# The tail of a chunked attention and eight-expert MoE kernel laid out by hand, with VectorE turning the rows of six experts

## The chip, the cores and the metric

The kernel runs on one NeuronCore of a Trainium2 chip. The metric is device time in microseconds (us) of one execution, as a median over runs. A profiled execution is one more, with a trace of every instruction; its span goes from the first to the last instruction.

Engines: PE is TensorE (PEld its weight loads), DVE is VectorE, ACT is ScalarE, POOL is GpSimd, SP is SyncE, which here issues DMAs.

## The reference

Two stages, all in float32. First a chunked linear attention with decay over 4 x 8 heads, 768 tokens, head size 32, state size 16, in chunks of 32 (cut to what matters):

```python
cum = np.cumsum(log_a_chunk)                       # per head
M = (Cc @ Bc.T) * exp(cum_i - cum_j) * causal
y = M @ xc + (Cc @ state) * exp(cum)
state = exp(sum(log_a)) * state + (Bc * exp(cum_last - cum)).T @ xc
```

Its output, 3072 tokens of 256 values, goes through a mixture of experts with top-1 routing, 8 experts of 256 x 1024 x 256, and a capacity of 768 tokens for each, in the order of the tokens:

```python
e = argmax(x @ w_gate); gate = softmax(x @ w_gate)[e]
pos = how many earlier tokens chose e               # dropped where pos >= 768
out = gate * (relu(x @ w1[e]) @ w2[e])              # 0 where dropped
```

## The kernel before, in words

All engines' programs are written out in order by `moe_kernel` under a manual schedule; waits come from the tiles that instructions share. There is no planner: an instruction's place in the source is its place in its engine's queue.

**Attention.** 24 tiles of 128 tokens (`TILES`), six to a batch. The loop `for k in range(TILES + 1)` is a software pipeline. In step k, VectorE multiplies the scores of tile k by the decays (`masked`, tile `mz`, L436); TensorE turns the rows of tile k-2 and computes their logits (`rows_of`, `stage_c`), then does the products of tile k-1 (`intra` L451, `inter` L462, evicted by ScalarE as `ys`, L464), the state of tile k+1 (`carry`, tile `dsp`, L390, scaled by VectorE as `dsm`, L393) and, at the top of the next step, `scores` (L430). GpSimd prepares `bpt` and `ct` two tiles ahead.

**Routing.** Tiles are routed in groups (`GROUPS = [4, 4, 4, 4, 3, 2, 2, 1]`). `route_1` (VectorE: maximum, one-hot choice), `route_2` (TensorE: position of each token within its expert, tile `pos`), `route_3` (VectorE: gate, slot, one-hot tiles `hot_a`, `hot_e`; SP stores the rows to `rows_d` in HBM), `hot` (GpSimd) and `listed` (TensorE, added up in `table`). `route_1` and `route_3` put their VectorE operations in the list `side`; `trickle` runs five a step, `flush` runs all at once. A group that ends from step `LATE - 1` = 21 on, or at `LEAD` = 12, is flushed. From `table`, `numbers` makes `who`: for each expert and place, the token's number.

**Lead.** The first 128 tokens of expert 0 come from the first 12 tiles. They are fetched during the loop (`lead_gather`), turned after it (`lead_turn`) and go through w1 in eight pieces (`lead_gemm`, L622); w2 follows in the expert part (L987), with the turn of expert 0's other rows inside it (`TURN`).

**Experts.** `experts("first", ...)`: expert 0 with 296 rows, then experts 1 to 7 with 424 each. GpSimd fetches the rows by `who` in blocks of 128 (`gather`, `fetch`, L160), two experts ahead, each block released by a matmul of GEMM2. `turned` has TensorE turn them (`turn`, L150, eight transposes), ScalarE and VectorE split them in a high and a low part (`xh`, `xl`). GEMM1 (`gemm1`, L881) and GEMM2 (`gemm2`, L900) multiply high and low parts three ways. The weights are loaded by SP (`load_weights`, L105, L107) into one raw buffer for w1 and one for w2, as soon as the previous expert's are split (`split_weights`, ScalarE L121 and VectorE L122), which happens beside GEMM2. `finish` and `put` turn the result back, scale it by the gate and scatter it (GpSimd, L934). Expert 7 uses `gemm2_by_token` (L958). Expert 0's w1 is split in steps 19 to 22 of the loop (`SPLITS`), four pieces of 512 columns, its w2 after it.

**Rare part.** Under `tc.If` (L1044), for tokens beyond a window of 424 rows an expert or beyond the capacity: the same functions with `rare` set. With the inputs used it is not entered.

Of the kernel before, what the change touches and what calls it, by code (L numbers as in the profile page):

```python
# [18 lines left out]
P = 128  # L19
# [5 lines left out]
E = 8  # L25
# [8 lines left out]
GROUPS = [4, 4, 4, 4, 3, 2, 2, 1]  # L34
LEAD = 12
LATE = 22
WARM = 19
LOT = 4
TURN = (1, 4)
SPLITS = (19, 20, 21, 22)  # L40
# [13 lines left out]
def moe_kernel(ctx, tc, a, x, bt, bn, cn, hd, w_gate, w1, w2, cb, out, cap):  # L54
# [11 lines left out]
    ks = -(-cap // P)  # L66

# [30 lines left out]
    win = min(WIN, cap)  # L98
# [11 lines left out]
    def split_weights(e, r1, r2, wp, cuts=2):  # L110
        t = {}
        todo = []
        for nm, r in (("1", r1), ("2", r2)):
# [4 lines left out]
            m = n * r.shape[2] // cuts  # L118
            for i in range(cuts):
                def job(hi=flat(hi), lo=flat(lo), r=flat(r), sl=slice(i * m, (i + 1) * m)):  # L120
                    act.activation(hi[:, sl], r[:, sl], AF.Copy)  # L121
                    dve.tensor_tensor(out=lo[:, sl], in0=r[:, sl], in1=hi[:, sl].bitcast(F32), op=ALU.subtract)  # L122
                todo.append(job)
            t[nm] = (hi, lo)
        wset[e] = t
        return todo
# [25 lines left out]

    def follow(ins, name, reason):
# [12 lines left out]
    def numbers(out, cols):  # L166
        dve.scalar_tensor_tensor(out=out, in0=table[:, 0, cols], scalar=float(P), in1=table[:, 1, cols], op0=ALU.mult, op1=ALU.add)


    with ExitStack() as at:  # L170
# [356 lines left out]
        def route_2(n0, T, rt, df, ep, oh, se, soon=False):  # L527
            flush()
            act.activation(ep, df, AF.Exp)
            pos = p1.tile([P, T, E], F32, name="pos", tag="y" if soon else "sp", bufs=1 if soon else 2)  # L530
            pe.matmul(pos, tri, oh.rearrange("p t e -> p (t e)"), start=True, stop=False)
            pe.matmul(pos, ones, bc(runs[0].rearrange("p (o e) -> p o e", o=1), [P, T, E]), start=False, stop=T == 1)
            for i in range(1, T):
                pe.matmul(pos[:, i:T], ones, bc(oh[:, i - 1:i], [P, T - i, E]), start=False, stop=i == T - 1)
# [80 lines left out]
        lead_f = list(range(NF if lead else 0))  # L615

        def lead_gemm(n):
            for _ in range(min(n, len(lead_f))):
                f = lead_f.pop(0)
                ps = p1.tile([P, lead], F32, name="lead_p1", tag=("yp0", "yp1", "lj")[f % 3])  # L620
                for k in range(2):
                    pe.matmul(ps, rw[0][:, k, f * P:(f + 1) * P], lead_t["x"][:, k], start=k == 0, stop=k == 1)  # L622
                act.activation(lead_t["h"][:, f], ps, AF.Relu)
# [14 lines left out]
        def settle_due(now):  # L638
            while due and due[0][0] <= now < TILES - 0.5:
                _, group = due.pop(0)  # L640
                route_3(*route_2(*group, soon=True))
                if now > LATE - 1 or group[0] + group[1] == LEAD:
# [10 lines left out]
        def lot_of(n):  # L653
            gi = max(i for i in range(len(GROUPS)) if starts[i] <= n)
            T, i = GROUPS[gi], n - starts[gi]
            if T <= 2:
# [20 lines left out]
        for k in range(TILES + 1):  # L677
            b, t = divmod(k, NT)
            n = k - 2
            if k < TILES:  # L680
                ms[k] = masked(sps.pop(k) if k in sps else scores(k), lxs.pop(k))
# [4 lines left out]
            def rows_of(n, k):  # L686
                gi, i, direct, size = lot_of(n)
                if i == 0:
                    T = GROUPS[gi]
                    rt = sm.tile([P, 6, ROW], F32, name="rt", bufs=3) if T > 2 else sm.tile([P, T, ROW], F32, name=f"rt{gi}", bufs=1)  # L690
                    grp[gi] = rt, sm.tile([P, 6, E], F32, name="L", bufs=3)[:, 0:T]
                stage_c(sb[n], grp[gi][0], i, grp[gi][1], direct)
                lot = None
                if size:
                    lot = [sb[m] for m in range(n + 1 - size, n + 1)], grp[gi][1][:, i + 1 - size:i + 1]
                for f in full:
                    group_done(f, k)
                full.clear()
                if n + 1 == starts[gi + 1]:
                    if not direct:  # L700
                        full.append(gi)
                    else:
                        group_done(gi, k)
                return lot

            if n >= 0 and k < TILES:
                lot = rows_of(n, k)
            if k + 1 < TILES:
                lxs[k + 1] = decays(k + 1)
            if k >= 1:  # L710
                yps, lots = intra(x_of(k - 1), ms.pop(k - 1), sa[k - 1], lot, hots)
            if k + 1 < TILES:
                dsm = carry(k + 1)
# [4 lines left out]
            if k == TILES:  # L718
                rows_of(n, k)
# [9 lines left out]
            if k + 1 < TILES:  # L729
                sa[k + 1] = advance(k + 1, dsm)  # L730
            if lead and k == TILES:
                lead_turn()
# [38 lines left out]

        rt = sm.tile([P, 1, ROW], F32, name="rt_last", bufs=1)
        lg = stage_c_last(sb.pop(TILES - 1), rt)
        ops = take()
        for _, group in due[:-1]:
# [346 lines left out]
```

## Time and profile before

| | |
|---|---|
| median of 3 runs | 292.1 us (290.39 to 294.04) |
| profiled execution | 292.75 us |
| its span | 291.0 us |
| mean granted TensorE clock | 0.939 |
| busy, share of the span | PE 89%, PEld 74%, DVE 60%, ACT 45%, POOL 37% |
| DMA | 36.40 MB, mean 125 GB/s |

The page gives the span in 40 slices, so 7.3 us each; a digit is a tenth, of busy time or of the granted clock. Other views cut the span in stretches, list single instructions in order of time (start, length, engine, source line, tiles written and read), follow the chain of waits back from the last instruction, or group instructions by line. Matmul lengths are modelled and overlap, so that a busy TensorE is not TensorE at its peak.

### The profile page before, as it was taken

What the parts mean: (1) busy time and instruction counts of PE and PEld (TensorE: products, weight loads), DVE (VectorE), ACT (ScalarE), POOL (GpSimd) and SP (SyncE); (2) the same over time, 40 slices, a digit from 0 to 9 for tenths busy, and PEclk for the clock granted to TensorE, in tenths of its full rate; (3) what the DMA queues carried; (4) which work ended last, traced back from release to release, by engine and by line L of the source; (5) the groups of instructions that cost most, each with busy time, mean ns of one, the idle gap of its engine ahead of it and who ended that gap; (6) DMA issues with size and microseconds to landing.
All of it is one profiled execution on the core that took longest, in us unless ns stands there. A gap on an engine that the chain in (4) does not pass through costs nothing.

```text
span 291.0 us, 7064 instructions
## 1 busy us (share of the span) xinstructions
PE 258.1 (89%) x2768; PEld 215.4 (74%) x2768; DVE 174.6 (60%) x461; ACT 129.6 (45%) x290; POOL 107.0 (37%) x151
## 2 busy tenths in 40 slices
PE   7669999997988869799999999999999999999910
PEld 2235566654557758699999999999998999999900
DVE  7678797865875663476746736646656656645100
ACT  2458566564632342374644544544644635432000
POOL 6972324415102041555244335225325424042410
PEclk9999999999965795999999999999999999999975
DMA  6774527759112154227074173182271461001100
GB/s 187 169 213 103 169 71 202 235 143 337 43 41 93 55 187 141 84 63 305 16 216 169 33 247 140 31 304 78 67 284 47 119 233 51 2 18 42 38 27 0
DMA packets 14374, 36.40 MB, mean 125 GB/s; under 512 B 4621, under 2 KB 7919, under 8 KB 12288
## 3 DMA queue, kind: packets, MB, share of 16 engines
q1 hardware_dynamic: 10928, 28.18, 30.5%
q0 software_dynamic: 3280, 7.71, 8.1%
q8 instruction: 23, 0.38, 0.6%
q14 instruction: 15, 0.12, 0.1%
q10 hardware_dynamic: 128, 0.01, 0.0%
HBM read 29.29 MB, written 6.63 MB: 123 GB/s over the span
## 4 chain that ended last, share of the span: by engine, by line
PE 75%; DVE 11%; DMA 4%; ACT 2%; issue 2%; POOL 1%; SPq 0%; POOLq 0%; DVEq 0%; ACTq 0%
PE ps L881 25%; PE ps L900 22%; PE ps2f L958 4%; PE ps L150 3%; PE yp L451 3%; DMA g<-rows_d,who 3%; PE sp L430 2%; PE psy L946 2%; PE yp L462 2%; PE pj L469 2%; DVE mz L436 2%; PE dsp L390 2%; PE lead_p L622 1%; DVE state L417 1%; PE ldp L380 1%
## 5 line engine op out<-in xcount | busy, mean ns | idle before, releaser
L884 DVE SCALAR_TENSOR_TENSOR hl<-ps,hh 128x424 fp32r<-128x424 f32 (+1 forms) x64 | 37.3, 583 | 43.7 <-ACT hh L883 36.6
L160 POOL DMA_INDIRECT g<-rows_d,who x31 | 34.1, 1099 | 55.5 <-PE ps L900 43.5
L883 ACT ACTIVATE hh<-ps 128x424 fp32r<-128x424 f32 (+1 forms) x64 | 32.7, 511 | 46.7 <-PE ps L881 45.9
L122 DVE TENSOR_TENSOR wl<-r,wh 128x1024 fp32r<-128x1024 f32 (+1 forms) x36 | 38.2, 1099 | 17.8 <-ACT wh L121 17.8
L934 POOL DMA_INDIRECT out<-yo,oi x31 | 30.5, 985 | 43.3 <-DVE yo L933 38.2
L900 PE MATMUL ps<-hh,wh 128*128 128x424 f32 (+1 forms) x112 | 39.5, 352 | 0.0
L900 PE MATMUL ps<-hh,wl 128*128 128x424 f32 (+1 forms) x112 | 39.0, 348 | 0.0
L900 PE MATMUL ps<-hl,wh 128*128 128x424 f32 (+1 forms) x112 | 38.9, 347 | 0.0
L881 PE MATMUL ps<-xh,wh 128*128 128x424 f32 (+1 forms) x128 | 37.5, 374 | 0.0
L881 PE MATMUL ps<-xh,wl 128*128 128x424 f32 (+1 forms) x128 | 34.7, 353 | 0.0
L881 PE MATMUL ps<-xl,wh 128*128 128x424 f32 (+1 forms) x128 | 34.6, 352 | 0.0
L121 ACT ACTIVATE wh<-r 128x1024 fp32r<-128x1024 f32 (+1 forms) x36 | 32.7, 956 | 0.1
L881 PEld LDWEIGHTS ps<-xh,wl 128*128 128x128 f32 x128 | 24.2, 193 | 0.6
L881 PEld LDWEIGHTS ps<-xl,wh 128*128 128x128 f32 x128 | 24.1, 192 | 0.6
L881 PEld LDWEIGHTS ps<-xh,wh 128*128 128x128 f32 x128 | 22.3, 196 | 0.3
L900 PEld LDWEIGHTS ps<-hh,wh 128*128 128x128 f32 x112 | 21.0, 188 | 1.0
L900 PEld LDWEIGHTS ps<-hh,wl 128*128 128x128 f32 x112 | 21.2, 189 | 0.4
L900 PEld LDWEIGHTS ps<-hl,wh 128*128 128x128 f32 x112 | 21.0, 187 | 0.3
L906 ACT ACTIVATE yt<-ps 128x424 f32<-128x424 f32 (+1 forms) x14 | 7.1, 509 | 29.7 <-PE ps L900 18.9
L464 ACT ACTIVATE ys<-yp 128x128 f32<-128x128 f32 x48 | 10.7, 275 | 20.0 <-PE yp L462 20.0
L355 POOL TENSOR_TENSOR bpt<-b_s,wt 128x128 f32<-128x128 f32 x22 | 9.3, 421 | 24.6 <-PE dsp L390 24.5
L451 PEld LDWEIGHTS yp<-mz,xz 128*32 128x32 f32 x768 | 13.3, 117 | 5.9 <-issue 2.2
(175 smaller groups left out, 455.6 us busy)
## 6 DMA issues: line engine op xcount, KB each, us to landing
r<-w SPq DMA_DIRECT2D x16, 1024.0 KB
rows_d<-rt SPq DMA_DIRECT2D x4, 514.0 KB
xz<-x SPq DMA_DIRECT2D x6, 256.0 KB
b_s<-bt SPq DMA_DIRECT2D x3, 384.0 KB
c_n<-cn SPq DMA_DIRECT2D x3, 384.0 KB
b_n<-bn SPq DMA_DIRECT2D x3, 384.0 KB
xz<-x SPq DMA_DIRECT2D x6, 128.0 KB
hd_s<-hd SPq DMA_DIRECT2D x1, 718.0 KB
```

Source lines behind the costliest of these rows:

```text
L121: act.activation(hi[:, sl], r[:, sl], AF.Copy)
L122: dve.tensor_tensor(out=lo[:, sl], in0=r[:, sl], in1=hi[:, sl].bitcast(F32), op=ALU.subtract)
L160: got = pool.indirect_dma_start(out=g[0:r, s], out_offset=None, in_=rows_d[0:known, :], in_offset=bass.IndirectOffsetOnAxis(ap=index[0:r, ...
L355: engine.tensor_tensor(out=bpt.rearrange("p (h n) -> p h n", n=N), in0=nat(b, "bt", t * P, (t + 1) * P).rearrange("p (h n) -> p h n", n=N) ...
L451: pe.matmul(yps[g][32 * hh:32 * hh + 32, c * CH:(c + 1) * CH], x_z[:, c, h * D:(h + 1) * D], m[:, h], start=c == 0, stop=False, skip_group ...
L464: act.activation(ys[:, g], yps[g], AF.Copy)
L881: mm = pe.matmul(ps, wv[:, k, fs], xv[:, k], start=i == 0, stop=i == 5)
L883: act.activation(hh[:, f, 0:w], ps, AF.Relu)
L884: dve.scalar_tensor_tensor(out=hl[:, f, 0:w], in0=ps, scalar=0.0, in1=hh[:, f, 0:w].bitcast(F32), op0=ALU.max, op1=ALU.subtract)
L900: mm = pe.matmul(ps, wv[:, f, ds], hv[:, f, 0:w], start=f == 0 and j == 0, stop=f == NF - 1 and j == 2)
L934: sc = pool.indirect_dma_start(out=out, out_offset=bass.IndirectOffsetOnAxis(ap=oi[0:r, s:s + 1], axis=0), in_=yo[0:r], in_offset=None, bo ...
L958: pe.matmul(ps, hv[:, f, sl], wv[:, f, :], start=f == 0 and j == 0, stop=f == NF - 1 and j == 2)
```

## The change

- **Loop and tail.** Groups become `[4, 4, 4, 4, 4, 3, 1]`; only the group that ends at `LEAD` is flushed. The loop ends with step 22. Step 23 and what follows is written out: tile 23's products first, then the routing of tiles 16 to 19, the turn of the lead rows, the routing of tiles 20 to 22 woven with that of tile 23, and `lead_gemm` in four places between (two pieces of w1 each, one eviction for both). The last tokens' lists are summed in one PSUM tile (`spots`) and added to what `table` held (`settled`).
- **Expert 0's weights** are loaded in step 10 instead of 16. Its w1 is split in 16 pieces of 128 columns, two in each of steps 14 to 21, by ScalarE and GpSimd; its w2 after the counts (`own`, `dead`) instead of ahead of them. The turn of expert 0's other rows comes behind the whole lead GEMM instead of inside it.
- **Experts 2 to 7.** After GEMM2 of expert u, SP stores the fetched rows of expert u+2 to a scratch tensor `xr_d` in HBM and reads them back as four quarters of 64 columns (`quarter`), so that a VectorE transpose of 32 x 32 blocks (`turned_blocks`) gives the turned rows; w1's rows are put in the matching order on input. One split of both halves follows. 448 rows are fetched instead of 424. Experts 0 and 1 are turned by TensorE as before.
- **Rare part.** `chosen` finds the rows by one-hot matmuls over all of `rows_d`, loaded by SP, in place of GpSimd's fetches.

```diff
-GROUPS = [4, 4, 4, 4, 3, 2, 2, 1]
+GROUPS = [4, 4, 4, 4, 4, 3, 1]
-SPLITS = (19, 20, 21, 22)
+SPLITS = range(14, 22)
...
+    def turned_blocks(x_t, g4):
+        dve.transpose(out=x_t.rearrange("p k (f i) -> p k f i", i=Q), in_=g4.rearrange("p f (k c) -> p k f c", k=2))
...
         def group_done(gi, k):
-            soon = k >= LATE - 1 or starts[gi + 1] == LEAD
             rt, L = grp.pop(gi)
             due.append((k + 1, route_1(starts[gi], GROUPS[gi], rt, L)))
-            if soon and k < TILES:
+            if starts[gi + 1] == LEAD:
                 flush()
...
-            if k == 2 * NT + 4:
+            if k == NT + 4:
                 rw = load_weights(0, raw)
             if k == SPLITS[0]:
-                wjobs = split_weights(0, *rw, wpool, 4)
+                wjobs = split_weights(0, *rw, wpool, (CUTS, 4), (pool, dve))
             if k in SPLITS:
-                wjobs.pop(0)()
+                for _ in range(CUTS // len(SPLITS)):
+                    wjobs.pop(0)()
...
+        settle_due(k + 1)
+        early = take()
+        lead_turn()
+        rows_of(k - 1, k)
+        mid = take()
...
+        for op in early:
+            op()
+        hots.extend(hot(*v, pool) for v in known)
+        numbers(settled, slice(0, E * ks))
+        weave(mid, [lambda: None, lambda: None] + late)
+        lead_gemm()
+        mid = route_2(*due.pop()[1], at_of(1, 4 * E)[:, 0:3 * E].rearrange("p (t e) -> p t e", e=E))
+        route_3(*mid)
...
+        weave(mid[3:], late)
+        hots.append(hot(*known[0], pool))
+        hots.append(hot(*known[1], dve))
+        while lead_f:
+            lead_gemm()
+        while hots:
+            list_(*hots.pop(0))
+        dve.tensor_tensor(out=who, in0=settled, in1=spots, op=ALU.add)
...
+            def quarter(u, g, w):
+                d, n = xr_d[u % 2], -(-w // Q) * Q
+                full = n // P * P
+                for lo, hi in ((0, full), (full, n)):
+                    if lo < hi:
+                        r = min(P, hi - lo)
+                        sp_.dma_start(out=d[lo:hi].rearrange("(s p) r -> p s r", p=r), in_=g[0:r, lo // P:-(-hi // P)])
+                g4 = gp.tile([P, n // Q, 64], F32, name="g4")
+                for q in range(4):
+                    sp_.dma_start(out=g4[q * Q:(q + 1) * Q], in_=d[0:n, q * 64:(q + 1) * 64].rearrange("(f i) c -> i f c", i=Q))
+                return g4
...
+                else:
+                    xt = gp.tile([P, 2, g4.shape[1] * Q], F32, name="xt", bufs=1)
+                    turned_blocks(xt, g4)
+                    act.activation(xh, xt[:, :, 0:w], AF.Copy)
+                    dve.tensor_tensor(out=xl, in0=xt[:, :, 0:w], in1=xh.bitcast(F32), op=ALU.subtract)
...
+                if u + 2 < len(units):
+                    four[u + 2] = quarter(u, ahead_g[u + 2], units[u + 2][2])
```

More of the change, by code (lines that the diff above doesn't have):

```diff
@@ L66, in moe_kernel @@
     ks = -(-cap // P)
+    win = min(WIN, cap)
+    quarters = -(-win // Q)
+    xr_d = [dram.tile([quarters * Q, ROW], F32, name=f"xr_d{i}") for i in range(2)]
     hd_s = const.tile([P, CFW + 384 + 3 * HW], F32, name="hd_s")
@@ L638, in settle_due @@
         def settle_due(now):
-            while due and due[0][0] <= now < TILES - 0.5:
+            while due and due[0][0] <= now:
                 _, group = due.pop(0)
-                route_3(*route_2(*group, soon=True))
-                if now > LATE - 1 or group[0] + group[1] == LEAD:
+                route_3(*route_2(*group))
+                if group[0] + group[1] == LEAD:
                     flush()
@@ L684, in moe_kernel @@
             lot = None
[L686 to L706, printed above, removed]
+            if n >= 0:
                 lot = rows_of(n, k)
-            if k + 1 < TILES:
-                lxs[k + 1] = decays(k + 1)
+            lxs[k + 1] = decays(k + 1)
             if k >= 1:
                 yps, lots = intra(x_of(k - 1), ms.pop(k - 1), sa[k - 1], lot, hots)
-            if k + 1 < TILES:
-                dsm = carry(k + 1)
+            dsm = carry(k + 1)
             if k >= 1:
@@ L728, in moe_kernel @@
                 hots.append(hot(*known.pop(0), pool))
[L729 to L732, printed above, removed]
+            sa[k + 1] = advance(k + 1, dsm)
             settle_due(k)
@@ L770, in weave @@
                         ops[i]()
-        rt = sm.tile([P, 1, ROW], F32, name="rt_last", bufs=1)
-        lg = stage_c_last(sb.pop(TILES - 1), rt)
-        ops = take()
-        for _, group in due[:-1]:
-            route_3(*route_2(*group))
-        flush()
-        side.extend(ops)
-        lead_gemm(1)
-        final = route_2(*due[-1][1])
-        last = route_last(TILES - 1, rt, lg)
-        ops = take()
-        route_3(*final)
-        weave(take(), ops)
-        lead_gemm(2)
-        last = route_2(*last)
+        k = TILES - 1
@@ new lines, in moe_kernel @@
+        sb[k] = inter(yps, cts.pop(k), sa.pop(k))
+        for f in lots:
+            f()
+        side.extend(early)
+        settle_due(k + 1)
+        early = take()
+        assert not due and not hots
+        if lead:
+            lead_turn()
+        rows_of(k - 1, k)
+        mid = take()
+        rt = sm.tile([P, 1, ROW], F32, name="rt_last", bufs=1)
+        lg = at_of(0, E)
+        for g in range(2):
+            pe.matmul(lg, sb[k][:, g], wg[:, g, 0:E], start=g == 0, stop=g == 1, skip_group_check=True)
@@ L787, in moe_kernel @@
+        last = route_last(k, rt, lg)
+        late = take()
+        pj = p1.tile([P, 512], F32, name="pj_last", tag="y")
+        turn_rows(pj, sb.pop(k))
+        act.activation(rt[:, 0, 0:DM], pj[:, 0:DM], AF.Copy)
+        for op in early:
+            op()
         hots.extend(hot(*v, pool) for v in known)
         known.clear()
-        route_3(*last)
-        flush()
-        hots.extend(hot(*v, dve) for v in known)
-        lead_gemm(3)
-        for v in hots:
-            listed(p1.tile([P, 2 * E * ks], F32, name="lst", tag="y"), *v)()
@@ L795, in moe_kernel, with list_ @@
-        numbers(who, slice(0, E * ks))
-        while len(lead_f) > 1:
-            lead_gemm(1)
+        settled = sm.tile([P, E * ks], F32, name="settled")
+        numbers(settled, slice(0, E * ks))
[3 more added lines that the diff above has]
+        route_3(*mid)
+        mid = take()
+        started = []
+        def list_(n0, T, a_, b_):
+            for i in range(T):
+                for v in range(2):
+                    pe.matmul(spots, a_[:, i], b_[:, i, v], start=not started, stop=(n0 + i, v) == (k, 1), skip_group_check=True)
+                    started.append(n0 + i)
@@ new lines, in moe_kernel @@
+        for op in mid[:3]:
+            op()
+        last = route_2(*last, at_of(2, E).rearrange("p (t e) -> p t e", t=1))
+        route_3(*last)
+        late = take()
+        while hots:
[4 more added lines that the diff above has]
+        hots.append(hot(*known[1], dve))
+        known.clear()
+        while lead_f:
+            lead_gemm()
+        while hots:
+            list_(*hots.pop(0))
+        dve.tensor_tensor(out=who, in0=settled, in1=spots, op=ALU.add)
@@ L844, in block @@
                 def block(s, *pace):
[L845 removed]
+                    fetch(g, who[:, e * ks + w0 // P:(e + 1) * ks], most, only=(s,), pace=pace)
                 return g, [lambda *pace, s=s: block(s, *pace) for s in range(blocks)]
             rows_ = []
[L850 removed]
+            def quarter(u, g, w):
[9 more added lines that the diff above has]
+                return g4
```

164 lines of the change are left out of this document (113 added, 51 removed).

## The prediction

> **What bounds the kernel now.** I read the page's clock line first, then the stretches (columns: stretch, length, busy us of PE, PEld, DVE, ACT, POOL, granted clock, DMA share, GB/s), cut where TensorE's work changes.
>
> ```profile
> PEclk9999999999965795999999999999999999999975
> ```
>
> ```profile
> 79.30:81.40 2.10, 0.00 (x0) 0.00 (x0) 1.93 (x9) 0.38 (x1) 0.97 (x2) 1.00 0.71 249
> 81.40:92.40 11.00, 10.53 (x188) 8.06 (x189) 7.65 (x36) 3.31 (x15) 1.68 (x4) 0.51 0.17 56
> 92.40:103.60 11.20, 9.10 (x58) 8.21 (x58) 5.82 (x39) 4.19 (x18) 1.01 (x5) 0.72 0.13 43
> 103.60:111.90 8.30, 6.35 (x39) 5.25 (x39) 4.99 (x20) 3.28 (x7) 3.53 (x3) 0.82 0.47 164
> 111.90:124.50 12.60, 10.46 (x61) 9.54 (x61) 4.49 (x12) 4.14 (x11) 5.11 (x5) 0.85 0.41 130
> 124.50:265.70 141.20, 141.20 (x776) 133.54 (x777) 87.15 (x152) 69.24 (x110) 54.41 (x53) 1.00 0.37 127
> 265.70:277.30 11.60, 11.52 (x97) 11.31 (x95) 2.15 (x6) 0.53 (x1) 2.95 (x3) 1.00 0.11 36
> 277.30:291.00 13.70, 0.00 (x0) 0.00 (x0) 0.43 (x1) 0.00 (x0) 0.93 (x1) 0.58 0.02 5
> ```
>
> Three limits. From 124.5 to 277.3 TensorE has no gap and full clock: only matmuls taken away shorten it. From 79.3 to 124.5 it stands still for 2.1 us and then runs at 0.51 to 0.85 of its clock. After 277.3 there is one scaling and one scatter, and 13 us pass. What opens the middle part is in the timeline; the bracket is the idle time and its releaser:
>
> ```profile
> 71.35 0.19 DVE L521 TENSOR_TENSOR df<-L,mx 128x32 f32<-128x32 f32 x1
> ...
> 79.65 0.97 POOL L583 TENSOR_TENSOR hot_b<-hot_e,cb_s 128x192 bf16<-128x192 bf16 x2 [3.26 <-DVE mx L520]
> 79.69 0.50 DVE L521 TENSOR_TENSOR df<-L,mx 128x24 f32<-128x24 f32 x1
> ...
> 81.44 0.55 PE L469 MATMUL pj<-hd_s,ys 128*128 128x128 f32 x2 [2.15 <-DVE dsm L393]
> ```
>
> VectorE does a group's routing (the flush in `group_done` from step LATE on) ahead of `dsm`, whose PSUM bank TensorE's next transposes need. TensorE idles 2.15 us and the clock halves.
>
> **The change, term by term.** Working is against the profiled execution, 292.75 us (span 291.0 and 1.75 around it); the median of the runs, 292.1, is 0.65 lower.
>
> *A, steps 20 to 23.* Only LEAD's group still flushes; the rest trickles. So the 2.1 us stall goes, and with it the drop of the clock. The same matmuls in the chain of waits, full clock and half:
>
> ```profile
> 56.77 0.58 PE yp L451 x32
> ...
> 65.14 0.40 PE yp L462 x16
> ...
> 72.94 0.59 PE sp L430 x8
> ...
> 83.40 1.01 PE yp L451 x32
> ...
> 84.84 0.65 PE yp L462 x16
> ...
> 85.69 1.06 PE sp L430 x8
> ```
>
> From 81.4 to 92.4 lie three, three and one of these: 3 x 0.43 + 3 x 0.25 + 0.47 = 2.5 us. The other 4.5 us of matmuls there shrink less (small ones); I take a quarter, 1.1. Together -3.6. What is late next is the ordinary step: about 3 us of TensorE.
>
> Added in steps 14 to 21: the split of expert 0's w1, now 16 pieces of 128 columns on ScalarE and GpSimd instead of four of 512 on ScalarE and VectorE.
>
> ```profile
> 73.07 0.62 ACT L121 ACTIVATE wh<-r 128x512 fp32r<-128x512 f32 x1
> ...
> 73.72 0.69 DVE L122 TENSOR_TENSOR wl<-r,wh 128x512 fp32r<-128x512 f32 x1 [0.46 <-ACT wh L121]
> ```
>
> ```profile
> L355 POOL TENSOR_TENSOR bpt<-b_s,wt 128x128 f32<-128x128 f32 x22 | 9.3, 421 | 24.6 <-PE dsp L390 24.5
> L623 ACT ACTIVATE lead_h<-lead_p 128x128 f32<-128x128 f32 x8 | 2.2, 278 | 4.7 <-PE cnt L801 2.2 <-PE lead_p L622 2.0 <-PE pos L532 0.6
> ```
>
> ScalarE: 16 x 0.278 = 4.4 against 4 x 0.62 = 2.5. VectorE loses 4 x 0.69 = 2.8. GpSimd gains 16 x 0.42 = 6.7, beside `bpt` and `ct`, which wait for it in its queue: `bpt` sat 24.5 us waiting for TensorE, so that queue has room. But `df` took 0.50 us instead of 0.19 while GpSimd ran `hot_b`: 0.3 per meeting. Price between -2.8 (VectorE's relief counts, ScalarE hides) and +16 x 0.3 + 1.9 = +6.7; I take +0.7, since VectorE is relieved as much as it is disturbed. The early load of w1 and w2 (step 10 instead of 16) queues on SP ahead of batch 3's loads, needed some 8 us later; 0.
>
> [...]
>
> A = -2.1 - 3.6 + 0.7 = **-5.0** (-8.5 to +1).
>
> *B, from tile 23's `ys` to the first row fetch.* Before:
>
> ```profile
> 92.37 0.45 ACT L464 ACTIVATE ys<-yp 128x128 f32<-128x128 f32 x2 [2.05 <-PE yp L462]
> ...
> 94.14 0.17 DVE L520 TENSOR_REDUCE mx<-L 128x2 f32<-128x16 f32 x1 [1.04 <-ACT L L474]
> ...
> 94.97 0.17 DVE L524 TENSOR_TENSOR oh<-cand,m 128x16 bf16<-128x16 f32 x1
> ```
>
> ```profile
> 59.90 0.21 DVE L567 TENSOR_REDUCE tot<-oh 128x8 f32<-128x32 bf16 x1
> ...
> 61.56 0.35 DVE L555 TENSOR_TENSOR hot_e<-cb_s,base 128x192 bf16<-128x192 bf16 x1
> ```
>
> ```profile
> 103.31 0.35 SPq L105 DMA_DIRECT2D r<-w  x1
> ```
>
> ```profile
> 103.56 5.11 DMA g<-rows_d,who
> ```
>
> That is 92.82 to 103.56, 10.7 us. The new order on VectorE: about 1.7 us until `held` of tiles 16 to 19, their `route_3` (59.90 to 61.91: 2.0), `route_1` of tiles 20 to 22 woven with tile 23's (94.14 to 95.14, 1.0 each: 2.0, and 0.5 for meetings with GpSimd's `hot`), three operations of 0.17, the two `route_3` woven (19 operations, 3.2), `hot` on GpSimd (0.97 for four tiles, about 1.0 here), eight matmuls and the one addition for `who` (0.7): 11.6 from tile 23's last matmul, 10.9 from `ys`. TensorE's faster clock doesn't help, because VectorE sets this part; `lead_gemm`'s pieces fill TensorE's gaps and are off the path. **0** (-1.5 to +1.5).
>
> *C, first fetch to expert 0's first matmul, 8.3 us.* w1 of expert 1 is asked for after the last `lead_gemm`, now some 3 us ahead of the fetch instead of 0.25, so the rows no longer queue behind it; the remaining limit is GpSimd issuing three fetches. The six matmuls left of the lead GEMM behind the turn are gone. The w2 split (four VectorE pieces, 2.8) moves behind `own` and `dead` into the wait for the rows. **-1.7** (-2.5 to 0).
>
> *D, GEMM1 of expert 0, 12.6 us at clock 0.85.* A mean of 0.85 is 3.8 us at half clock, 1.9 to win at most; whether the gap before it halves the clock again I can't tell, so half of that: **-1.0** (-1.9 to 0).
>
> *E, rows of experts 2 to 7.* TensorE's turns and the GEMM2 by which I time them:
>
> ```profile
> 141.10 1.17 PE ps L150 x8
> ...
> 162.89 9.48 PE ps L900 x48
> ...
> 182.55 1.17 PE ps L150 x8
> ...
> 244.89 1.17 PE ps L150 x8
> ```
>
> Six turns, 6 x 1.17 = 7.0 us off a TensorE without gaps. In their place, per expert: a VectorE transpose of 2 x 448 columns, one split of 2 x 424 (0.8 ScalarE, 0.9 VectorE, scaled from w's rows) for two of 0.5 to 0.6 each. No row shows a VectorE transpose; at the split's pace of one column per ns it is 1.0, at four times that 4. VectorE idles 54 of the 141 us here, near 8 per expert, so even 4 fits.
>
> The cover is the SP queue. Rows are stored to `xr_d`, read back in four loads of 256-byte pieces, and only behind them the next weights.
>
> ```profile
> 171.51 1.03 POOL L160 DMA_INDIRECT g<-rows_d,who  x1 [1.35 <-PE ps L900]
> ```
>
> ```profile
> 171.72 0.33 SPq L107 DMA_DIRECT2D r<-w  x1
> ```
>
> ```profile
> 176.00:177.00 1.00, 1.00 (x8) 0.97 (x7) 0.61 (x2) 0.52 (x1) 0.42 (x1) 1.00 0.12 45
> ```
>
> Count from GEMM2's start T (162.89). The last fetch is issued by T+9.7 and lands by T+11.3 (13.3 if slow); storing 460 KB at 249 GB/s (the pace of the 512 rows stored in 79.3 to 81.4) takes 1.9, and I put 1 for its start: T+14.2. Those 512 rows kept the DMA engines 0.71 busy for 2.1 us, 1.5 of full work; so the four loads, 1792 pieces of as many bytes in all as 448 rows, take between 1.3 (by bytes) and 5.2 (by pieces), plus 2 for issue and start: T+17.5 to 21.5. A weight took from 171.72 until the DMAs were quiet, about 176.2: 4.5, 1 of it the start. Queued behind, w1 lands at T+21 to 25 and w2 at T+24.5 to 28.5. Before, w2 was there at T+13.3. VectorE is free for the turn at T+20.9 and GEMM1 starts at T+29.1: w1 must land by about T+26, w2 by T+29 (ScalarE's split of w2 stands ahead of `hh`, and three PSUM banks give 3.5 us). It fits, with 0.5 to 4.5 us over. **-6.5** (-7 to +8).
>
> *F, the end.* The rare branch loses its row fetches, the only DMAs that GpSimd issued in it. By source line:
>
> ```profile
> L1044 POOLq INC_SWDGE_SEM  x1: 1660/1660/1660, 282.4 to 282.4; - x1
> ```
>
> ```profile
> L1118 POOLq DRAIN  x3: 46/109/6028, 284.1 to 290.7; - x3
> ```
>
> GpSimd, not taking the branch, makes up for its DMAs' semaphores (1.66 us), then drains for 6.03; all engines wait. The first has nothing left to do: **-1.7**. The drain I leave: 73 DMAs of GpSimd stay as they were, 83 ns each; -6 if it followed from the first.
>
> **Sum:** -5.0 + 0 - 1.7 - 1.0 - 6.5 - 1.7 = -15.9; 292.75 - 15.9 = 276.85, and on the median's scale **276.2 us**.
>
> **The rivals.**
> - *The drain goes too*, or clock and D come out at their best ends. For: the drain starts right behind the semaphore instruction. Against: it has 73 entries of its own. 276.2 - 6 = 270. Chance 0.18.
> - [...] For: 2.15 us of idleness was enough, and B leaves TensorE half idle for 7 us. Then C and D are 0 and A loses 3: 276.2 + 5.7 = 282. Chance 0.18. [...]
> - *Rows turned late.* The loads at the slow end or a slow store: 1.5 us of waiting per expert takes E to +2: 285. Chance 0.12.
> - *Slower than before: weights late behind the row store on SP.* One mechanism: at twice the store's price per piece, 10.4 us for the loads, w2 lands at T+33.7, 4.7 past its limit, and each of six experts waits: 276.2 + 28 = 304. It decides from 2.7 us past the limit (15.9 / 6), so at loads of 8.4 us. Against: 256-byte pieces should cost less than 1028-byte ones, not more. Chance 0.06.
>
> The forecast itself has 0.46. A measurement here tells about 2% (5.8 us) from no change. Faster than 286.3: the forecast, the first two rivals and part of the third, with some held back for what I haven't seen: 0.86; within 2%: 0.08; slower: 0.06. The range, leaving out the last rival and the first one's extremes: 267 to 286.
>
> **What would show it.** A: clock 1.00 through step 23, `mz` of tile 23 near 83.5 instead of 88.64. B: VectorE without gaps there. E: no `ps L150` rows between GEMM1 and GEMM2 after expert 1's, a cycle of 19.7 instead of 20.8, DMA quiet before GEMM1. F: no INC_SWDGE_SEM. Wrong if ScalarE or VectorE waits for `r` or `g4` while TensorE idles, or the clock line shows as many low slices as now.

## The result and the profile after

The changed kernel takes **279.1 us** (median of four runs, 276.4 to 280.9) against 291.6 (four runs, 290.4 to 294.0); the ratio is 0.953, with a 95% interval of 0.943 to 0.964. Some executions of a kernel are over 1.5% longer than its fastest; the ratios leave them out, and of the traces below only that of rows1_free is of such a one. The forecast was 276.2 in a range of 267 to 286. The profiled execution took 278.61 us with a span of 276.8, so 14.1 us less than the profiled execution of before (292.75); the prediction's sum was 15.9.

The stages don't agree with their terms as well as the sum does. First the clock line of the page of the changed kernel, then VectorE's `mz` (the masked scores, one per tile) of tiles 12, 16 and 23 in the timeline of before, and of the changed kernel:

```profile
PEclk9966999999999998699999999999999999999996
```

```profile
47.95 0.69 DVE L436 TENSOR_TENSOR mz<-sp,lx 128x512 f32<-128x512 f32 x1
61.83 0.68 DVE L436 TENSOR_TENSOR mz<-sp,lx 128x512 f32<-128x512 f32 x1
88.64 0.69 DVE L436 TENSOR_TENSOR mz<-sp,lx 128x512 f32<-128x512 f32 x1
```

```profile
50.52 0.69 DVE L442 TENSOR_TENSOR mz<-sp,lx 128x512 f32<-128x512 f32 x1
67.67 0.68 DVE L442 TENSOR_TENSOR mz<-sp,lx 128x512 f32<-128x512 f32 x1
87.97 0.69 DVE L442 TENSOR_TENSOR mz<-sp,lx 128x512 f32<-128x512 f32 x1 [0.46 <-PE sp L436]
```

The low slices of 80 to 100 us are gone. From tile 16 to tile 23 it takes 20.3 us instead of 26.8, so 6.5 won. But tile 16 comes 5.8 us later than before: 2.6 of it by tile 12, and 3.3 between tiles 12 and 16 (17.15 us instead of 13.88). Two low slices now stand near the start, and two at the hand-over to the experts.

The hand-over from the scan to the experts, in the changed kernel's timeline (start, length, engine; the bracket is the idle time and its releaser): the last `ys`, the row fetches on GpSimd, w2 of expert 1 on SP, the turn of expert 0's rows, and the first matmuls of expert 0's two products:

```profile
90.82 0.45 ACT L470 ACTIVATE ys<-yp 128x128 f32<-128x128 f32 x2 [0.52 <-PE yp L468]
101.17 1.43 POOL L166 DMA_INDIRECT g<-rows_d,who  x1 [2.42 <-DVE lead_oi L862]
102.90 1.42 POOL L166 DMA_INDIRECT g<-rows_d,who  x1 [0.30 <-issue]
103.50 0.33 SPq L110 DMA_DIRECT2D r<-w  x1
104.62 0.99 POOL L166 DMA_INDIRECT g<-rows_d,who  x1 [0.30 <-issue]
108.92 1.61 PE L153 MATMUL ps<-hd_s,g 128*128 128x128 f32 x5 [3.79 <-DMA g<-rows_d,who]
110.46 1.19 PE L973 MATMUL ps<-xh,wh 128*128 128x296 f32 x2
119.75 0.98 POOL L166 DMA_INDIRECT g<-rows_d,who  x1 [0.30 <-PE ps L973]
122.40 0.92 PE L153 MATMUL ps<-hd_s,g 40*128 40x40 f32 x5 [0.63 <-DMA g<-rows_d,who]
123.25 0.41 PE L992 MATMUL ps<-hh,wh 128*128 128x296 f32 x1
```

The first fetch is at 101.17 instead of 103.56, yet the first product begins 9.3 us later instead of 8.3, and the second product again waits for rows. In stretches (columns as in the prediction: stretch, length, busy us of PE, PEld, DVE, ACT, POOL, granted clock, DMA share, GB/s):

```profile
110.50:123.30 12.80, 10.90 (x60) 9.68 (x59) 5.25 (x16) 4.28 (x10) 5.09 (x5) 0.82 0.16 44
123.30:262.00 138.70, 138.70 (x777) 134.00 (x777) 94.37 (x154) 69.49 (x105) 63.13 (x54) 1.00 0.53 171
```

The first product still runs at 0.82 of the clock. After it TensorE has no gap, now without the turns. The end, by the chain of waits and by source line: the last scaling starts at 267.80, and the drain of 6.03 us follows without the semaphore instruction.

```profile
267.80 0.49 DVE yo L1025
```

```profile
L1215 POOLq DRAIN  x3: 46/109/6034, 269.9 to 276.5; - x3
```

| stage | before | after | change | forecast |
|---|---|---|---|---|
| A: to the end of tile 23's `ys` | 92.8 | 91.3 | -1.5 | -5.0 |
| B: to the first row fetch | 10.7 | 9.9 | -0.8 | 0 |
| C: to expert 0's first product | 8.3 | 9.3 | +1.0 | -1.7 |
| D: to its second product | 12.5 | 12.8 | +0.3 | -1.0 |
| E: to the last matmul | 152.8 | 144.5 | -8.3 | -6.5 |
| F: to the end of the span | 13.7 | 9.1 | -4.7 | -1.7 |

Each row compares one execution with one other. The trace of rare_only below has the old code up to the last matmul and ends tile 23's `ys` at 89.8 us instead of 92.8, so a difference in A of a few us need not be the change's.

### The profile page after: what moved, and what is told of

Its sections match the earlier page's. It is cut to its first block, busy times and chain, and to the rows that moved or that the text cites. A ratio compares the mean times of both kernels' runs of the same rounds, so it can differ in the third digit from the quotient of the medians.

```text
span 276.8 us, 7022 instructions
## 1 busy us (share of the span) xinstructions
PE 246.9 (89%) x2727; PEld 205.7 (74%) x2727; DVE 176.6 (64%) x438; ACT 129.9 (47%) x289; POOL 121.6 (44%) x165
## 4 chain that ended last, share of the span: by engine, by line
PE 77%; DVE 9%; DMA 4%; issue 3%; ACT 2%; POOL 1%; SPq 0%; POOLq 0%; DVEq 0%; ACTq 0%
PE ps L973 27%; PE ps L992 22%; PE yp L457 4%; PE ps2f L1050 4%; PE sp L436 4%; DMA g<-rows_d,who 3%; PE yp L468 3%; PE pj L475 2%; PE psy L1038 2%; PE dsp L396 2%; PE ldp L386 2%; DVE mz L442 1%; PE yp L406 1%; DMA c_n<-cn 1%; PE lead_p L631 1%
## 5 line engine op out<-in xcount | busy, mean ns | idle before, releaser
L166 POOL DMA_INDIRECT g<-rows_d,who x31 | 42.0, 1355 | 43.3 <-PE ps L992 30.9
L124 ACT ACTIVATE wh<-r 128x1024 fp32r<-128x1024 f32 (+2 forms) x48 | 34.4, 768 | 6.5 <-DMA r<-w 5.9
L125 DVE TENSOR_TENSOR wl<-r,wh 128x1024 fp32r<-128x1024 f32 (+1 forms) x32 | 35.3, 1148 | 3.3 <-ACT wh L124 3.2
L973 PEld LDWEIGHTS ps<-xh,wh 128*128 128x128 f32 x128 | 22.3, 195 | 0.7 <-ACT xh L935 0.3
L470 ACT ACTIVATE ys<-yp 128x128 f32<-128x128 f32 x48 | 10.7, 274 | 19.9 <-PE yp L468 19.9
L442 DVE TENSOR_TENSOR mz<-sp,lx 128x512 f32<-128x512 f32 x24 | 16.5, 687 | 4.5 <-PE sp L436 3.5
```

Of the source, the lines that this page charges most:

```text
L125: engine.tensor_tensor(out=lo[:, sl], in0=r[:, sl], in1=hi[:, sl].bitcast(F32), op=ALU.subtract)
L166: got = pool.indirect_dma_start(out=g[0:r, s], out_offset=None, in_=rows_d[0:known, :], in_offset=bass.IndirectOffsetOnAxis(ap=index[0:r, ...
L442: dve.tensor_tensor(out=m.rearrange("p (g h) i -> p g h i", g=2), in0=sp[:, :, 0:4 * CH].rearrange("p g (h i) -> p g h i", h=4), in1=lx.re ...
L973: mm = pe.matmul(ps, wv[:, k, fs], xv[:, k], start=i == 0, stop=i == 5)
```

## The experiments

Each row below is one kernel: the median of its runs, the ratio to the kernel before with its interval, and six stretches of its trace in us: `mz` of tile 12 to 16, 16 to 23, first fetch to first product (C), first to second product (D), first matmul of expert 1 to the last one, and from there to the end. The medians come from four sets of runs, in which the kernel before took 291.6 to 293.9 us, so medians of different sets compare only to some 2 us; each ratio is to the kernel before of its own set. In the four kernels with the old tail C is 7.3 to 8.4 and D 11.5 to 12.5, so single traces differ by 1 us there without a change of code.

| kernel | median | ratio | 12-16 | 16-23 | C | D | experts 1-7 | end |
|---|---|---|---|---|---|---|---|---|
| before | 291.6 to 293.9 | 1 | 13.9 | 26.8 | 8.3 | 12.5 | 146.2 | 13.7 |
| changed | 279.1 | 0.953 | 17.2 | 20.3 | 9.3 | 12.8 | 137.9 | 9.1 |
| rare_only | 287.6 | 0.985 (0.976-0.994) | 13.2 | 26.2 | 7.3 | 11.5 | 146.4 | 9.2 |
| no_flush_a | 293.2 | 1.002 (0.998-1.006) | 13.2 | 25.7 | 8.0 | 11.8 | 146.2 | 13.6 |
| early_load | 294.4 | 1.005 (0.999-1.011) | 17.0 | 26.4 | 8.4 | 12.4 | 146.4 | 11.5 |
| pe_turns | 289.4 | 0.985 (0.975-0.994) | 17.3 | 22.8 | 8.9 | 12.9 | 146.4 | 9.1 |
| split_dve | 283.4 | not formed | 17.5 | 22.3 | 9.8 | 12.8 | 137.9 | 9.3 |
| w2_step16 | 278.7 | 0.951 (0.939-0.964) | 17.6 | 20.3 | 10.1 | 12.7 | 138.1 | 9.1 |
| load16 | 275.8 | 0.950 (0.940-0.961) | 13.2 | 20.3 | 9.3 | 12.7 | 138.6 | 9.1 |
| w2_split_late | 281.1 | 0.963 (0.951-0.974) | 17.4 | 20.3 | 6.1 | 17.3 | 138.3 | 9.1 |
| rows1_free | 276.8 | 0.944 (0.931-0.957) | 16.7 | 20.6 | 11.6 | 10.9 | 139.0 | 9.1 |
| rows_ahead | 271.6 | 0.933 (0.920-0.945) | 16.8 | 20.3 | 6.1 | 10.1 | 138.7 | 9.1 |
| rows_load16 | **268.7** | **0.927 (0.916-0.939)** | 13.9 | 20.2 | 6.4 | 10.5 | 138.0 | 9.1 |
| rows_load16_warm | 269.0 | 0.925 (0.917-0.934) | 14.3 | 20.2 | 7.5 | 10.1 | 137.9 | 9.1 |

### What the end is worth: rare_only

The kernel before, with the changed kernel's `chosen` in the rare part (rows picked by matmuls with one-hot matrices) and without the rare part's fetches.

> The kernel before with one part of the change: the rare part builds its rows by matmuls and no longer by row fetches. Theory from the two traces: the stretch from the last matmul to the end shrinks from 13.8 us to about 9.0, because with the 1.66 us semaphore instruction also the 3.4 us go that GpSimd spends ahead of it after its branch; the 6.03 us drain stays. Time: before minus 4.7 us. Rival one, the prediction's step F: only the 1.66 us go, before minus 1.7. Rival two: the shorter end of the changed kernel comes from another part of the change, and this run shows 13.8 us as before, no change in time.

By source line, GpSimd's branch in the kernel before:

```profile
L1044 POOLq COMPARE_BRANCH  x1: 74/74/74, 279.4 to 279.4; - x1
```

Last matmul to end: 13.7 became 9.2, as the traces of the change itself show, so this part alone is worth 4.5 us between these traces. Before, 3 us lay between GpSimd's branch (279.4) and the semaphore instruction (282.4), and they go with it. In early_load's trace, with the same code, those 3 us were 1.1 and the end was 11.5: some 2 us of the 4.5 vary between executions. The DMA packets in the traces say what these 2 us are likely to be: in the kernel before, two 8 KB packets of instructions land by 280.6, and GpSimd's next instruction starts at 281.95, 1.3 us behind them (no_flush_a: 279.0 and 280.4); in early_load no such packet lies between, and it starts 0.4 us behind the branch.

### What the flush is worth: no_flush_a

The kernel before:

```
-            soon = k >= LATE - 1 or starts[gi + 1] == LEAD
+            soon = starts[gi + 1] == LEAD
```

> The kernel before with one condition changed: the first routing operations of the late groups are no longer put on VectorE at once, they trickle between the scan's operations (only the group of the lead expert still flushes). Theory of the prediction's step A: the 2.15 us stall of TensorE ahead of tile 22's transposes goes, the clock stays at 1.00 until the last tile, and mz of tile 23 starts near 84 instead of 88.64; what the tail does with it is open, so the time is 2 to 4.5 us under before. Rival: the clock halves in steps 20 to 23 for another reason (the many short gaps there), mz of tile 23 stays above 87, and the time is within 1 us of before.

The waits of TensorE from 75 to 95 us (us in total, times, longest), and a stretch behind them:

```profile
PE pos L531 <- DVE oh L524: 1.8, 1, 1.8
...
PE pj L469 <- DVE dsm L393: 0.4, 1, 0.4
```

```profile
91.60:95.00 3.40, 3.40 (x19) 3.34 (x20) 1.49 (x12) 1.04 (x4) 0.00 (x0) 0.50 0.02 5
```

The 2.15 us stall at `dsm` shrinks to 0.4, and a stall of 1.8 us appears a step later: TensorE's `pos` needs `oh`, the last of the operations that now trickle, because `route_2` begins with a flush of its own. The clock still halves, from 91 us on. Steps 16 to 23 win 1.1 us, not the 6.5 of the whole change, and the time stays. The rival's outcome holds, though its reason, many short gaps, is not shown: one wait took the place of the other. The flush of these groups alone was not what held steps 20 to 23.

### Where tile 16's delay comes from: early_load, w2_step16, load16

The kernel before, with the load moved as in the change:

```
-            if k == 2 * NT + 4:
+            if k == NT + 4:
                 rw = load_weights(0, raw)
```

> The kernel before with one statement moved: the two weight loads of expert 0 are issued at step 10 instead of 16, as in the changed kernel. In the trace of the changed kernel mz of tile 16 starts 5.9 us later than before: 2.2 us from a half clock in steps 2 to 4, and 2.5 us around a TensorE stall of 1.9 us at 55.7 us that no engine released. Theory one: the loads' traffic at 48 to 58 us makes that stall; then this run shows a TensorE stall of 1.5 us or more with no releaser between 48 and 60 us, mz of tile 16 near 64.5 instead of 61.83, and a time about 2.5 us over before. Theory two: both belong to that one execution and not to the change; then mz of tile 16 starts within 0.8 us of 61.83 and the time is that of before within 1 us.

TensorE's waits from 45 to 70 us in this run ("issue": nothing that the profile shows):

```profile
PE sp L430 <- issue: 1.5, 1, 1.5
PE yp L462 <- issue: 1.4, 1, 1.4
```

The same stretch of the changed kernel, its longest wait and then its load:

```profile
PE sp L436 <- issue: 1.9, 1, 1.9
```

```profile
46.00:50.00 4.00, 3.81 (x104) 2.72 (x108) 2.62 (x10) 3.01 (x10) 2.52 (x6) 1.00 0.94 267
...
54.00:58.00 4.00, 2.10 (x63) 1.13 (x52) 1.81 (x6) 0.86 (x4) 0.83 (x2) 1.00 0.98 376
```

Theory one holds: one moved statement in the old kernel makes tile 12 to 16 take 17.0 us, and TensorE stands still at the same matmuls as in the changed kernel. The eight kernels that load at step 10 take 16.7 to 17.6 there, the six that load at step 16 13.2 to 14.3. In the time of the old kernel little of it is left (ratio 1.005, 0.999 to 1.011): in this trace the way from tile 16 to the first row fetch is 3.0 us shorter than before, and the clock is halved for 6.8 us of it instead of 17.1.

What TensorE waited for is in the traces' DMA packets. The page of the changed kernel lists a queue with 22 packets of instructions, 16 KB each:

```profile
q8 instruction: 22, 0.36, 0.5%
```

They fit TensorE's 5537 instructions, some 250 to a packet. In all eight kernels that load at step 10, TensorE stands still 1.3 to 2.2 us behind the same 1985 instructions of the trace; in early_load and pe_turns a second time, exactly 256 instructions later. Each of these stalls ends 1.3 to 1.6 us after such a packet has landed: in the changed kernel the packet is under way from 55.17 to 56.07 us, and TensorE goes on at 57.55. The packet sets out 3.2 to 4.3 us after TensorE has begun the 256 instructions before, in the six kernels that load at step 16 0 to 2.3 us after, and there TensorE doesn't stall. So beside the weight load TensorE's own instructions come late. It is the length of the full stretch that differs: in slices of 2 us the DMA engines of early_load are over 0.9 busy from 46 to 60 us, those of the kernel before from 52 to 56.

Then the changed kernel with half of the load moved back, and with all of it:

```
-        sp_.dma_start(out=r2.rearrange("p f d -> p (f d)"), in_=w2[e])
+        if not later:
+            sp_.dma_start(out=r2.rearrange("p f d -> p (f d)"), in_=w2[e])
...
-                rw = load_weights(0, raw)
+                rw = load_weights(0, raw, True)
...
+            if k == 2 * NT + 4:
+                sp_.dma_start(out=rw[1].rearrange("p f d -> p (f d)"), in_=w2[0])
```

> The changed kernel, with only w1 of expert 0 loaded at step 10 and w2 (first needed at 99 us) at step 16, where the kernel before had both. In the changed kernel the DMA engines are 0.94 to 0.99 busy from 46 to 62 us, TensorE stands 1.9 us at 55.7 and 0.6 us at 63.1 with no releaser, and mz of tile 12 to mz of tile 16 takes 17.15 us; before, and in two variants of it that load at step 16, it took 13.1 to 13.9. Theory (the early load meets batch 3's loads): with half of it moved, the stretch takes 13.5 to 15.5 us and the time falls by 1.5 to 3.5 us. Rival: the stretch is longer because of the pieces of the split in steps 14 and 15, then it stays at 17 and so does the time.

```profile
54.00:58.00 4.00, 1.94 (x9) 0.93 (x9) 0.84 (x3) 0.00 (x0) 0.07 (x1) 0.75 1.04 341
```

17.6: nothing won. One megabyte keeps the DMA engines as full until 58 us, and TensorE is busy 1.94 of 4 us; its instructions land at 54.61, and it goes on at 56.06. The rival's reason is excluded by early_load, which has no pieces of the split in those steps.

```
-SPLITS = range(14, 22)
+SPLITS = range(19, 23)
-            if k == NT + 4:
+            if k == 2 * NT + 4:
```

> The changed kernel with both weight loads of expert 0 back at step 16 and its w1 split, still 16 pieces on GpSimd, in steps 19 to 22, four a step. Theory (1 MB beside batch 3's loads is enough to stall TensorE, so the load has to lie behind them): mz of tile 12 to mz of tile 16 takes 13 to 14 us instead of 17.2, and steps 19 to 23 get dearer by the crowded pieces, 11.6 us from mz of tile 19 to that of tile 23 becoming 12 to 14; the time falls by 1.5 to 3.5 us. Rival: the crowded pieces give it all back (ScalarE 1.1 and GpSimd 1.7 us more per step), mz of tile 23 starts no earlier against mz of tile 0, time within 1 us or up.

```profile
48.00:61.20 13.20, 12.95 (x353) 8.03 (x352) 11.36 (x44) 8.09 (x25) 4.35 (x10) 1.00 0.60 175
```

13.2 us, with the DMA engines at 0.60; and the split in four steps costs nothing (16 to 23 stays at 20.3). The median is 3.3 us under the changed kernel's, though the two ratios, from different sets of runs, overlap; rows_ahead and rows_load16 below, which differ by this edit and ran together, are 271.6 and 268.7.

### The first split: split_dve

```
-                wjobs = split_weights(0, *rw, wpool, (CUTS, 4), (pool, dve))
+                wjobs = split_weights(0, *rw, wpool, (CUTS, 4), (dve, dve))
```

> The changed kernel with the subtractions of expert 0's w1 split on VectorE instead of GpSimd (16 of 128 columns, still in steps 14 to 21). In the changed kernel mz of tile 16 to mz of tile 23 takes 20.3 us. Theory one (GpSimd's pieces lock VectorE out more than they relieve it): it falls below 19.5 us. Theory two (VectorE sets these steps, and 16 pieces of 0.2 to 0.3 us are added to it): it rises by 2 to 5 us, and the time by as much. The prediction's step A put the sum of both effects at 0.7 us for the pieces on GpSimd against four on VectorE.

The same stretch, tile 16 to 23, of this run and of the changed kernel:

```profile
68.00:90.40 22.40, 18.65 (x453) 11.33 (x445) 16.16 (x57) 12.36 (x46) 6.91 (x15) 0.92 0.26 75
```

```profile
67.70:88.00 20.30, 17.33 (x453) 10.63 (x449) 13.91 (x45) 12.25 (x46) 13.00 (x30) 1.00 0.31 89
```

Theory two's outcome: 2.0 us longer, VectorE 2.25 us busier, and the clock drops (0.92), which may be part of the 2.0. GpSimd's pieces are the better place. Beside operations of GpSimd, VectorE's `state` took up to 0.54 us in the changed kernel instead of 0.28, `mz` 0.68 to 0.69 as without them.

### Rows and weights: w2_split_late, rows1_free, rows_ahead, rows_load16

The changed kernel, with the split of expert 0's w2 moved into its first product:

```
-        for j in wjobs:
-            j()
+        held_jobs.extend(wjobs)
...
                 for f in range(NF):
...
+                    if held_jobs and f % 2:
+                        held_jobs.pop(0)()
                     if f >= 1 and after:
```

> The changed kernel with the split of expert 0's w2 moved from ahead of the first row fetches into expert 0's first product (one piece after every second block). So VectorE is idle while GpSimd issues the fetches, and w2 of expert 1, which needs the same buffer, is asked for only after the split. In the changed kernel the fetches were issued at 101.17, 102.90 and 104.62 with that load at 103.50, the rows were in at 108.88, and the first product began at 110.46: 9.3 us. Theory: the rows wait behind that 1 MB load and the issues are slowed by 0.4 us twice; then from first fetch to first product 6.5 to 7 us, and the time falls by 2 to 3 us. Rival: the fetches set this themselves (in the kernel before it was 8.3 us), then it stays over 8.3 and the time within 1 us. Second rival: the split delays the first product by as much as is won.

```profile
99.86 1.09 POOL L167 DMA_INDIRECT g<-rows_d,who  x1 [2.62 <-DVE lead_oi L863]
...
105.91 0.95 PE L973 MATMUL ps<-xh,wh 128*128 128x296 f32 x2
...
116.68 0.33 SPq L111 DMA_DIRECT2D r<-w  x1
...
121.84 1.42 PE L154 MATMUL ps<-hd_s,g 40*128 40x40 f32 x5 [3.53 <-DMA g<-rows_d,who]
```

C falls from 9.3 to 6.1: the theory. But the load now goes out at 116.68, right behind the last fetch of expert 1's rows (116.16), and those rows are in only at 121.8, 5.6 us after the issue; in the changed kernel the last ones took 2.6. D grows to 17.3 (1.0 us of it because that fetch is issued later, counted from the first product, GpSimd's issues taking 1.3 to 1.5 us beside the split), and the time is 2 us up.

The other edit alone:

```
+                if u == 0:
+                    while rows_:
+                        rows_.pop(0)()
                 hh, hl = gemm1(e, w, xh, xl, after, by_token, u == 0)
```

> The changed kernel, where GpSimd issues expert 1's four row fetches right behind expert 0's three, without waiting for blocks of the first product. In the changed kernel the last of them is issued at 119.75 while the first product ends at 119.7, and the second product of expert 0 begins at 123.25: TensorE idles 2.6 us for rows. Theory: the rows are there, the time between the two products falls from 3.7 to about 1.3 us (a turn), and the time falls by 2.4 us, more where the gap would have halved the clock. Rival: the first rows now share the DMA engines with four more fetches and the weight load and arrive later by as much, so the start of the first product moves from 110.5 to about 112.5 and nothing is won.

D falls to 10.9 and C grows to 11.6: theory and rival both, with 2.4 us won in the median. (TensorE's waits for rows between the products are 1.8 us in the changed kernel, not 2.6.) Then both, and both with load16's edit:

> The changed kernel with both earlier edits of the tail: the split of expert 0's w2 inside its first product, and expert 1's rows fetched right behind expert 0's. Alone, the first brought first fetch to first product from 9.3 to 6.05 us, but the rows of expert 1 then waited behind the 1 MB load that it had put off (12.8 us from first to second product became 17.3); the second alone brought that to 10.9 but the start of the first product from 9.3 to 11.6. Theory (whatever rows are asked for after a weight load wait for it): together the load comes behind all rows, so 6 to 7.5 us and 10.9 to 12.5 us, 3.5 to 5 us under the changed kernel, about 275. Rival: seven fetches in a row delay each other, then the first part stays over 9 us and the time is that of the second edit alone, 276.8.

> Both of these: the tail with rows ahead of weights, and the loads at step 16. If the two act in different places the gains add up: 5 to 8 us under the changed kernel, 271 to 274. If the time up to the first fetch is set by the routing and not by the scan's steps, only the first counts: about 275.

The hand-over of rows_load16:

```profile
95.90 1.07 POOL L167 DMA_INDIRECT g<-rows_d,who  x1 [2.38 <-DVE lead_oi L863]
...
102.30 1.19 PE L973 MATMUL ps<-xh,wh 128*128 128x296 f32 x2
103.82 0.98 POOL L167 DMA_INDIRECT g<-rows_d,who  x1 [0.30 <-issue]
...
111.56 1.34 PE L154 MATMUL ps<-hd_s,g 128*128 128x128 f32 x8
112.83 0.41 PE L994 MATMUL ps<-hh,wh 128*128 128x296 f32 x1
113.50 0.33 SPq L111 DMA_DIRECT2D r<-w  x1
```

Seven fetches in a row, none slowed (0.98 to 1.07 us each), the turn of expert 1 without a wait, the weight load behind all rows. rows_ahead is 271.6 us, rows_load16 **268.7** (six runs, 268.0 to 271.1): 10 us under the changed kernel by the medians of two sets, 7.6 by the ratios (0.927 and 0.953 of some 292 us), and 25 under the kernel before of its own set. The gains add up, though rows_ahead won 7.5 us where 3.5 to 5 were expected (5.8 by the ratios): C and D together fell by 5.9.

### The clock of the first product: rows_load16_warm

```
+            for i in range(10):
+                warm = ph.tile([P, 384], F32, name="warm", tag="ps1")
+                pe.matmul(warm, cb_s[:, 0:128], cb_s[:, 0:384], start=True, stop=True)
             cur = turned(g, *first)
```

> The kernel with rows ahead of weights and the loads at step 16, and in addition ten matmuls of 128 x 384 on a constant, into a bank that nobody reads, between the lead expert's second product and the turn of expert 0's rows, where TensorE stood idle 2.4 us or more. Theory (the idle time before the rows is what halves the clock in expert 0's first product): the granted clock stays 1.00 through that product, and the stretch from its start to its end shrinks by 1.5 to 2 us, the time by as much. Rival: the clock halves anyway, since the ten matmuls take only 1.7 us of the gap, and the time is the same or 0.5 us longer.

No gain in the time. In its profile the clock was lost earlier, while TensorE worked: the lead expert's matmuls took 5.20 us here, at a granted clock of 0.50 from 92 to 96 us, and 2.92 in the changed kernel (the last row).

```profile
91.86 5.20 PE L632 MATMUL lead_p<-lead_h,r 128*128 128x128 f32 x24
```

```profile
95.87 2.92 PE L631 MATMUL lead_p<-lead_h,r 128*128 128x128 f32 x24
```

The first product took 10.1 us instead of 10.5, but the turn came 1.1 us later. Undecided: the experiment didn't hold the clock, so it can't say what holding it is worth.

### The turns: pe_turns

The changed kernel with `NATURAL = 8`, so that no expert's rows go through `quarter`.

> The changed kernel with one part undone: the rows of experts 2 to 7 are turned by TensorE again, with no store to and reads from memory in between. Theory from the two traces: from the first matmul of expert 0's second product to the last matmul 144.5 us become 152.8 again (six turns of 1.27 us from start to start, and 0.1 us for each of seven second products), so 8.3 us more than the changed kernel, about 287.4. Rival, the prediction's step E: 1.17 us each and part of it hidden, 6.5 us more, about 285.6. Rival two: the stretch was shorter for another reason (expert 0 and 1), then less than 4 us come back.

Expert 1 to the end of the last product takes 146.4 us, as in the kernel before (146.2), against 137.9: 8.5 us for six turns. The median rises by 10.3. This trace also shows 2.5 us more in tiles 16 to 23 and 1.5 in expert 0's second product, both at a half clock (0.52 from 62 to 69 us, 0.53 from 123.6 to 127) that the edit doesn't touch, so that the rest of the 10.3 need not be the turns'.

## Why the prediction was right, and where its steps were not

**A** (-5.0, measured -1.5). The clock of 1.00 through tile 23 came, and from tile 16 on the gain is 6.5, more than the 5.7 forecast ahead of the split's 0.7. That the flush caused the stall was too simple: taken away alone it moves the stall by one step. What the new groups, the written-out order and the split's new place give of the 6.5, no run separates, but for the 2.0 of split_dve. What failed is "the early load queues on SP ahead of batch 3's loads, needed some 8 us later; 0". The queue on SP was not the matter; the full DMA engines brought TensorE's instructions late: +3.3 us, shown by early_load and taken back by load16. The other 2.6 us by tile 12 are 2.2 of half clock in steps 2 to 4 and a few tenths, in an execution and not in the change: the same stretch of the changed kernel and of pe_turns, which has the same code there:

```profile
14.00:28.00 14.00, 13.03 (x210) 6.72 (x209) 8.98 (x25) 7.52 (x19) 6.95 (x12) 0.63 0.61 167
```

```profile
14.00:28.00 14.00, 11.60 (x273) 6.23 (x272) 11.15 (x32) 9.33 (x24) 7.80 (x14) 1.00 0.60 152
```

How far -5.0 was from the mark, one pair of executions can't say: in load16, with the load at step 16 and a clock of 1.00 through tile 23, `ys` of tile 23 ends at 84.8, which is 8.0 us ahead of the kernel before and 5.0 ahead of rare_only, whose scan is the old one.

**B** (0, measured -0.8). Inside its bounds, but not for its reason. "VectorE sets this part" with `lead_gemm` "off the path" is not what the chains of waits show, first before, then in the changed kernel:

```profile
95.98 0.85 PE lead_p L622 x4
...
96.89 1.90 PE lead_p L622 x8
...
98.82 1.44 PE lead_p L622 x12
```

```profile
96.03 2.77 PE lead_p L631 x24
```

`lead_gemm` is on the path in both, and so the clock counts. Before, it stood at half until 98.6 us; rare_only, with the same code and the full clock here, takes 8.8 us instead of 10.7. The changed kernel needs 9.9 at full clock, and its variants at full clock 9.9 to 10.5, so the new order is some 1 us longer than the old one at the same clock, as far as one trace of the old one can tell. That the sum came out near 0 is luck.

**C** (-1.7, measured +1.0). "The rows no longer queue behind w1" is true, and failed because the next load stands there: w2 of expert 1 waits until the lead expert's second product and the split of expert 0's w2 have read its buffer. The last subtraction of the split ends at 103.44, and the load goes out at 103.50, ahead of the last fetch. The rows of the second fetch land 6.0 us after its issue; those of rows_load16's first three, with no load issued among them, 2.5 to 3.5. I had followed only one of the two DMAs that `load_weights` issues. The split of w2, moved "into the wait for the rows", begins at 100.95, before the fetches, and GpSimd's first two issues take 1.43 and 1.42 us beside it, 1.09 and 1.00 in w2_split_late without it. With both out of the way, C is 6.1.

**D** (-1.0, measured +0.3). The clock was halved again (0.82 over this stretch), from 108.2 us on, near the end of TensorE's wait in C; that the wait causes it was not shown, since rows_load16_warm didn't hold the clock. And at the end of the first product TensorE waits 1.8 us for expert 1's rows (2.1 before), which I had not looked at. So D came out as in the rival of 282 us, where C and D are 0; the 3 us that it takes from A were not lost to the clock, which was 1.00 from tile 16 to tile 23.

**E** (-6.5, measured -8.3). The mechanism was right and the cover held; a turn was sized by its own 1.17 us, while from start to start it cost 1.27, and the second products beside it take 0.1 less each, for a reason that no run settles. The cover, for the cycle whose second product begins at T = 159.08:

```profile
159.08 0.35 PE L992 MATMUL ps<-hh,wh 128*128 128x424 f32 x1
171.68 1.56 SPq L899 DMA_DIRECT2D xr_d<-g  x2
174.93 1.96 SPq L902 DMA_DIRECT2D g<-xr_d  x4
180.69 1.11 DVE L157 STREAM_TRANSPOSE xt<-g 128x896 f32<-128x896 f32 x1 [0.79 <-DMA g<-xr_d]
183.26 2.01 ACT L124 ACTIVATE wh<-r 128x1024 fp32r<-128x1024 f32 x2 [0.51 <-DMA r<-w]
186.81 2.01 ACT L124 ACTIVATE wh<-r 128x1024 fp32r<-128x1024 f32 x2 [1.13 <-DMA r<-w]
```

The rows are there at T+21.6 (forecast 17.5 to 21.5), w1 at T+24.2 (21 to 25), w2 at T+27.7 (24.5 to 28.5): the slow end of each, 1.8 and 1.3 us inside the limits of T+26 and T+29.

VectorE's transpose, bounded between 1.0 and 4 us, took 1.11 for 896 columns, 0.8 of a column per ns. The time lies at the lower bound that I had from the split.

**F** (-1.7, measured -4.7). The semaphore instruction went and the drain stayed, as forecast; the 3 us ahead of it stood in the stretch that I quoted (13.7 us from 277.3 on with hardly any work in it), and I priced only the two instructions with a duration. Some 2 of these 3 us vary between executions (rare_only above).

So the range held in part by luck, because errors of both signs met: +3.5 (A), +2.7 (C) and +1.3 (D) against -0.8 (B), -1.8 (E) and -3.0 (F).

## What to carry to other kernels

A megabyte of weights is not free because its consumer is far off: ask which small, urgent transfers are under way in the microseconds after it is issued, rows and an engine's own instructions among them, and put it behind them. Follow every DMA of a moved step to the time at which its buffer lets it go. And when a sum of terms comes out right, compare the terms: here they led to 8 to 10 us that the total hid.

## What the runs showed of the hardware that was not expected

TensorE can run out of its own instructions. With the DMA engines over 0.9 busy for 10 us and more, it stood still 1.3 to 2.2 us around steps 13 and 14 in every kernel that loaded weights there, always behind the same 1985 instructions and until 1.3 to 1.6 us after a 16 KB packet of instructions had landed. The profile books such a wait as "issue".

The clock halves in executions where TensorE has no long gap: ahead of the 5.20 us row above (rows_load16_warm) its longest wait from 80 to 98 us was 0.4 us, while in the kernel before the clock halved behind a gap of 2.15 us. The same code ran steps 2 to 4 at full clock in one execution and at half in another (1.00 in pe_turns and 0.63 in the changed kernel, from 14 to 28 us). Inside the spans the stretches at half clock last 3.4 us (no_flush_a, 120.2 to 127 us), 6.8 and 17.1 (before) or 6.8 and 10.2 (changed), whole multiples of 3.4.
